# The last product of an mLSTM and feed-forward kernel: 256 tokens from seven products of halves for the second half of the tokens

## The chip, the cores and the metric

The kernel runs on one core of one Trainium2 chip. The metric is the device time of an execution in microseconds; smaller is better. A core has five engines that run their own instruction streams: PE (matrix products), DVE (vector), ACT (scalar), POOL (GpSimd) and SP (which here only issues DMAs). They wait for each other through semaphores.

## The reference

The input is q, k, v and an output gate of 4 batches x 8 heads x 768 tokens x 40, and two gates per token and head. An mLSTM cell is run over time, and its output, read as 3072 tokens of 320 features, goes through a multiplicative feed-forward net. All is in fp32.

```python
m_new = np.maximum(f_gate[:, :, t] + m, i_gate[:, :, t])
C = f_stab[:, :, None, None] * C + i_stab[:, :, None, None] * np.einsum('bhd,bhe->bhde', vt, kt)
h_tilde = np.einsum('bhde,bhe->bhd', C, qt)
denom = np.maximum(np.abs(nq), 1.0)
y[:, :, t] = o * h_tilde / denom
...
a = x @ w1            # x: 3072 x 320, w1 and w2: 320 x 1024
b = x @ w2
h = a * b @ w3        # 1024 x 1024
return (h @ w_out)    # 1024 x 320
```

## The kernel before

**Tiling.** The cell is worked in 24 chunks n of 128 tokens (n counts the four batches first, then time). A chunk is worked by step s = n: `quarter_work` makes the scores, the state products and, one step later, the outputs. The feed-forward net works on groups `gr` of four chunks, 512 tokens, six groups in all. `x_t[gr]` holds a group's cell output with features on the partitions. From `w3` and `w_out` the kernel first makes their product `w3o` (1024 x 320, as 8 slices of 128 rows; `w3_mm`), so that what is left of the net is (x w1 * x w2) w3o.

**The stages of the net.** For groups 0 to 2 `up` makes the products with w1 and w2 directly. For groups 3 to 5 `up_by_seven` makes them for 512 tokens by a scheme that needs seven products of halves in place of eight, with sums of the halves of the weights (`weight_sums`, on POOL, in steps 16 and 17) and of the tokens (`token_sums`, on DVE, line 647). It has four parts: `single` (three products per weight, line 674), `shared` (the other four, line 681, with copies by ACT, lines 688 and 690, and additions by DVE, lines 672, 670 and 697), `left` (the last 64 features and four additions by DVE, the "left additions", lines 670 and 672) and `product` (a times b, line 715). The result is `ab_t[gr]`, two tiles of 8 slices x 256 tokens, features on the partitions.

**The last product.** `ffn_out` (line 719) makes 128 tokens of the output: eight products of 128 x 128 weights (a slice of `ab_t`) with 320 columns of `w3o`, in one PSUM bank; ACT copies the bank (line 727) and issues the DMA to the output (line 729). There are 24 such blocks (`downs`).

**What sets the order.** The order is written out by hand. A loop runs over 32 steps; the lists `n_up`, `n_seven` and `n_down` say how many of the net's pieces each step holds:

```python
n_up = [0] * 2 + [1] * 4 + [2] * 10 + [0] * 16
n_seven = [0] * 19 + [1] * 12 + [0]
n_down = [0] * 16 + [2] * 5 + [1] * 9 + [0, 5]
```

Steps 0 to 23 carry the cell as well; step 24 (`s == NU`) finishes the last chunk's output; steps 25 to 31 hold the net alone. In steps 19 to 24 PE's order is `single`, `shared`, the blocks of `ffn_out`, `left`, then the cell's work; in steps 25 to 30 it is `shared`, `ffn_out`, `single`, `left`. PE's order is pinned (`in_order`), and the other engines work their streams in the order in which the compiler has put them, which follows the program's closely. On DVE a step runs: additions of `shared`, left additions, the cell's output for the chunk before (`outputs`, lines 412 to 434), `product`, the transpose of a chunk of x that has come back from DRAM (`x_turn`, line 461), and the transposes of the keys and queries of the chunk after (`turn`, line 313; they read the buffers `gates` and `q_all`, which the SP queue fills).

**PSUM.** Until step 24 two tiles of two banks each, `cell0` and `cell1`, belong to the cell and are lent to `shared`; four banks in rotation (`ps_m`) serve the rest. After step 24 the cell's banks are given to a second pool, and all eight go round in turn (`mps`): a product waits until the bank's last reader is done.

**Buffers.** `kbuf` (4 tiles), `vbuf` (5), `q_all` and `gates` hold the cell's inputs, and are not used after the last chunk. `pw` is a ring of five tiles for the cell's weights. `wo` is used again as `kept`, the intermediate sums of `up_by_seven`.

Of the kernel before, what the change touches and what calls it, by code (L numbers as in the profile page):

```python
# [8 lines left out]
FP = mybir.dt.float32  # L9
U32 = mybir.dt.uint32  # L10
AF = mybir.ActivationFunctionType
OP = mybir.AluOpType
# [4 lines left out]
def kernel(  # L17
# [26 lines left out]
    nc = tc.nc  # L44

    B, H, S, D = q.shape
# [30 lines left out]
    def mps(shape, name):  # L77
        pool = banks.pop(0)
        banks.append(pool)
        return pool.tile(shape, FP, name=name, tag="m")  # L80
# [29 lines left out]
    q_all = const.tile([P, NBQ * H * DP], FP, name="q_all")  # L110
    qbuf = [q_all[:, i * H * DP:(i + 1) * H * DP].rearrange("p (h d) -> p h d", d=DP) for i in range(NBQ)]
    kbuf = [const.tile([P, H, DP], FP, name=f"kbuf{i}") for i in range(NB)]
    vbuf = [const.tile([P, H, D1], FP, name=f"vbuf{i}") for i in range(NBV)]
    ident = const.tile([P, P], FP, name="ident")
    state = [[const.tile([P, NP, D1], FP, name=f"state{b}_{i}") for i in range(3)] for b in range(B)]
    aT = const.tile([P, NT2, BH], FP, name="aT")
# [132 lines left out]
    def fold():  # L249
        while ready_w3:  # L250
            w3_mm(ready_w3.pop(0))
        ready_w3.extend(turned_w3)
        turned_w3.clear()
# [465 lines left out]
    def ffn_out(blocks, pos=None):  # L719

        pos = pos or [mps([P, DM], "po") for _ in blocks]
        for (gr, j), po in zip(blocks, pos):
            for f in range(FO):
                mm(po, ab_t[gr][j // 2][:, f, j % 2 * P:(j % 2 + 1) * P], w3o[:, f, :], start=(f == 0), stop=(f == FO - 1))
        for (gr, j), po in zip(blocks, pos):
            o_sb = ffn.tile([P, DM], FP, name="o_sb", tag="o_sb", bufs=2)
            nc.scalar.copy(out=o_sb, in_=po)  # L727
            t0 = j * S + gr * P
            nc.scalar.dma_start(out=out[t0:t0 + P, :], in_=o_sb)


    ups = [(gr, [f, f + 1], slice(j * 2 * P, (j + 1) * 2 * P)) for gr in range(3) for j in range(2)
           for f in range(0, FO, 2)]
    downs = [(gr, j) for gr in range(NG) for j in range(GT)]
    sevens = [(gr, f) for gr in range(3, NG) for f in range(FH)]
    n_up = [0] * 2 + [1] * 4 + [2] * 10 + [0] * 16
    n_seven = [0] * 19 + [1] * 12 + [0]
    n_down = [0] * 16 + [2] * 5 + [1] * 9 + [0, 5]
    w12 = [("w12", i, part) for part in range(2) for i in range(2 * KF + 1)]
    todo = w12[5:] + [("wo", i, 0) for i in range(FO)] + [("w3", ko, part) for ko in range(FO) for part in range(2)]  # L740
    n_cvt = [0, 0, 2, 0, 1, 2, 3, 3, 3] + [2] * 6
# [5 lines left out]
    for s in range(len(n_up)):  # L747
# [28 lines left out]
        while s >= N_DVE and turned < min(s - 2, NY):  # L776
            x_trans(turned)
            turned += 1
        fold()
        seven = None  # L780
        if n_seven[s]:
            seven = up_by_seven(*sevens.pop(0), (lambda i: cell[i // 2][:, i % 2].rearrange("p (i t) -> p i t", i=2)) if s <= NU else
# [4 lines left out]
        if seven and s <= NU:  # L787
            ffn_out([downs.pop(0) for _ in range(n_down[s])], [cell[1][:, i, 0:DM] for i in range(2)])
        else:
            for _ in range(n_down[s]):  # L790
                ffn_out([downs.pop(0)])
        if seven and s > NU:
            seven[0]()
        now = [ups.pop(0) for _ in range(n_up[s])]
# [38 lines left out]
        with tc.issue_after(gated.ins) if gated else nullcontext():  # L833
            if seven:
                seven[3]()
            if NY <= s - 2 < NU:
                x_turn(s - 2)
            for n in () if s == 1 else (s + 2,) if s < B else (s + 2, s + 3) if s == B else (s + 3,):
                if n < N_U:
                    rows_of_u(n)  # L840
            if N_DVE <= s + 1 < NU:
                gated = turn(s + 1)
            if s - 2 in range(4 * GT - 1, NU, GT):
                token_sums((s - 2) // GT)
        if s == 0:
            weighted(1)
            weights(1)
            masks(1)
            gate_cols(g, gT, nc.scalar.copy)
# [37 lines left out]
            for ins in keep_order(front):  # L887
                behind.enter_context(tc.issue_after(ins))
    behind.close()
    assert not ups and not sevens and not downs and not todo and not pend and not turned_w3 and not ready_w3, (len(ups), len(downs), len(todo), len(pend))  # L890
# [1 line left out]
_INS = ['q', 'k', 'v', 'i_gate', 'f_gate', 'o_gate', 'moe_w1', 'moe_w2', 'moe_w3', 'moe_w_out']  # L892
_OUTS = [((3072, 320), 'float32')]
# [25 lines left out]
```

## Time and profile before

| | us |
|---|---|
| median of 3 executions | 436.54 (435.71 to 437.29) |
| the profiled execution | 436.73 |
| its span, first to last instruction | 435.0 |
| mean granted PE clock in it | 0.984 of full speed |
| PE busy | 421.6 (97%) |
| DVE busy | 306.3 (70%) |
| ACT busy | 151.8 (35%) |
| POOL busy | 92.8 (21%) |
| the products of `ffn_out` (po and cell<-w3o,ab) | 70.6 + 35.4 of PE |

Busy time is the time in which an engine works on an instruction; its share is over the whole span. A row of the profile names the line of the kernel, the engine, the operation, output<-inputs by the program's names and, in brackets, the idle time ahead of it with what ended it. An fp32 product appears as two records on PE, each with its own weight load on the row PEld. Records of PE overlap: the pace of a stream is read from starts, not from durations. The span ends with the last output DMA.

The steps are found by their products: step 20 lies at 264.8 to 283.4 us of the span, step 21 to 297.7, step 22 to 312.0, step 23 to 326.2, step 24 to 339.6, step 25 to 352.0; steps 26 to 29 take 12.43 each, step 30 ends at 409.9, and step 31 is the rest.

### The profile page before, as it was taken

How to read it: one execution, taken by the hardware profiler on the slowest of the kernel's cores; microseconds unless marked ns; L12 is line 12 of the kernel's file. 1: busy time of each engine (PE TensorE's matmuls, PEld its weight loads, DVE VectorE, ACT ScalarE, POOL GpSimd, SP SyncE). 2: the span in 40 equal slices, each digit the busy share in tenths (PEclk: the TensorE clock that was granted, in tenths of full speed). 3: DMA queues.
4: the chain of work that ended last, by engine and by line, in shares of the span. 5: the costliest groups of instructions: out<-in, count | busy, mean ns of one | idle time of the engine just before them, and what ended most of it. 6: DMA issues, size and time to landing. Idle time of an engine off the chain costs nothing.

```text
span 435.0 us, 12730 instructions
## 1 busy us (share of the span) xinstructions
PE 421.6 (97%) x5233; PEld 335.1 (77%) x5233; DVE 306.3 (70%) x633; ACT 151.8 (35%) x409; POOL 92.8 (21%) x163
## 2 busy tenths in 40 slices
PE   7699899999999999999999999999999999999996
PEld 6688778878788787887777778788777777777774
DVE  6756886778949778777746968698998876444800
ACT  4866563566724523530332203123211111110110
POOL 4530342333303203303317623022100000000000
PEclk9979799999999999999999999999999999999999
DMA  8999977498987776884426676746221110000001
GB/s 186 213 183 232 222 111 131 126 198 169 205 197 134 171 174 141 173 168 92 102 63 135 151 130 145 160 98 137 53 54 37 35 35 15 17 17 15 2 30 46
DMA packets 135211, 51.14 MB, mean 118 GB/s; under 512 B 109360, under 2 KB 126960, under 8 KB 135152
## 3 DMA queue, kind: packets, MB, share of 16 engines
q1 hardware_dynamic: 131552, 46.29, 51.7%
q10 hardware_dynamic: 3600, 4.03, 2.7%
q8 instruction: 41, 0.67, 0.7%
q14 instruction: 18, 0.15, 0.1%
HBM read 44.50 MB, written 5.80 MB: 116 GB/s over the span
## 4 chain that ended last, share of the span: by engine, by line
PE 71%; SPq 8%; issue 8%; DMA 5%; POOL 3%; DVE 2%; ACT 1%; POOLq 0%; DVEq 0%; ACTq 0%
PE cell L92 19%; PE pa L92 19%; PE pb L92 12%; PE po L92 10%; PE wp L92 6%; PE p L92 5%; SPq L135 4%; DMA raw<-in_moe_w_dram 3%; SPq L180 2%; POOL pw L304 1%; POOL raw L645 1%; SPq L149 1%; SPq L144 1%; DVE w3T L652 1%; PE pt L95 1%
## 5 line engine op out<-in xcount | busy, mean ns | idle before, releaser
L92 PE MATMUL po<-w3o,ab 128*128 128x320 f32 x256 | 70.6, 433 | 0.0
L92 PEld LDWEIGHTS po<-w3o,ab 128*128 128x128 f32 x256 | 48.4, 190 | 19.7 <-issue 0.4
L92 PE MATMUL pa<-xT,w 128*128 128x256 f32 x240 | 61.5, 387 | 1.6 <-ACT xT L475 1.6
L331 POOL TENSOR_TENSOR state<-state,decay 128x164 f32<-128x164 f32 x40 | 19.7, 493 | 168.9 <-DVE state L395 139.2
L92 PEld LDWEIGHTS pa<-xT,w 128*128 128x128 f32 x240 | 45.3, 194 | 9.5 <-ACT xT L475 2.1
L299 ACT ACTIVATE pw<-pw,aT 128x64 f32<-128x64 f32 x184 | 46.4, 339 | 3.3 <-ACT o_sb L727 1.9
L304 POOL TENSOR_SCALAR_AFFINE_SELECT pw<-pw 64x512 f32<-64x512 f32 x48 | 38.2, 796 | 37.0 <-ACT pw L299 24.7
L92 PE MATMUL pb<-xT,w 128*128 128x256 f32 x192 | 45.4, 379 | 0.0
L92 PEld LDWEIGHTS pb<-xT,w 128*128 128x128 f32 x192 | 36.5, 190 | 5.0
L92 PE MATMUL pa<-xT,wr 64*64 64x256 f32 x384 | 37.0, 386 | 0.5 <-DVE wr L196 0.5
L92 PE MATMUL pb<-xT,wr 64*64 64x256 f32 x384 | 36.4, 380 | 0.0
L92 PE MATMUL wp<-wo,w3T 128*128 128x320 f32 x128 | 35.9, 433 | 0.2
L624 ACT ACTIVATE a_sb<-pa 128x512 f32<-128x512 f32 x24 | 14.3, 596 | 61.5 <-PE pb L92 61.5
L92 PE MATMUL cell<-w3o,ab 128*128 128x320 f32 x128 | 35.4, 432 | 0.0
L625 DVE TENSOR_TENSOR ab<-pb,a_sb 128x512 f32<-128x512 f32 x24 | 16.4, 686 | 25.8 <-ACT a_sb L624 25.7
L727 ACT COPY o_sb<-po 128x320 f32<-128x320 f32 x16 | 6.8, 426 | 74.4 <-PE po L92 74.4
L92 PEld LDWEIGHTS cell<-w3o,ab 128*128 128x128 f32 x128 | 24.3, 190 | 9.5
L672 DVE SCALAR_TENSOR_TENSOR a_sb<-pa,wo 128x512 f32<-128x512 f32 x12 | 8.3, 690 | 32.6 <-PE pa L92 32.6
L92 PEld LDWEIGHTS wp<-wo,w3T 128*128 128x128 f32 x128 | 23.8, 190 | 9.6 <-DVE ab L625 0.4
L92 PEld LDWEIGHTS pa<-xT,wr 64*64 64x64 f32 x384 | 18.9, 132 | 15.4 <-issue 8.8
L419 DVE TENSOR_TENSOR h<-cell,h 64x164 f32<-64x164 f32 x88 | 28.7, 326 | 1.7
L92 PEld LDWEIGHTS pb<-xT,wr 64*64 64x64 f32 x384 | 20.1, 133 | 3.0
(141 smaller groups left out, 730.4 us busy)
## 6 DMA issues: line engine op xcount, KB each, us to landing
raw<-in_moe_w_dram SPq DMA_DIRECT2D x64, 128.0 KB, 3.2
kbuf<-in_k_dram SPq DMA_DIRECT2D x24, 160.0 KB, 4.2
vbuf<-in_v_dram SPq DMA_DIRECT2D x24, 160.0 KB, 4.7
o_in<-in_o_gate_dram SPq DMA_DIRECT2D x24, 160.0 KB, 4.8
out_dram<-o_sb ACTq DMA_DIRECT2D x24, 160.0 KB, 1.8
pw<-U_d SPq DMA_DIRECT2D x28, 128.0 KB, 3.6
raw<-in_moe_w_dram SPq DMA_DIRECT2D x5, 512.0 KB, 6.8
raw<-in_moe_w_out_dram SPq DMA_DIRECT2D x8, 320.0 KB, 3.8
```

The lines of the kernel that those rows point to most:

```text
L92: in_order(nc.tensor.matmul(out, lhsT=lhsT, rhs=rhs, start=start, stop=stop))
L95: in_order(nc.tensor.transpose(out, in_, ident[0:n, 0:n]))
L135: nc.sync.dma_start(out=dst, in_=rows(src, n))
L180: nc.sync.dma_start(out=dst, in_=src)
L299: nc.scalar.activation(out=pw[:, h, :], in_=src[:, h, :], func=AF.Exp, bias=aT[:, c, b * H + h:b * H + h + 1])
L304: nc.gpsimd.affine_select(out=pw[r], in_=pw[r], compare_op=OP.is_ge, fill=0.0, base=0, pattern=[[0, H], [1, L]], channel_multiplier=-1)
L331: nc.gpsimd.tensor_tensor(out=new, in0=old, op=OP.mult, in1=decay[:, b * NP:(b + 1) * NP, 2 * c + x:2 * c + x + 1] .to_broadcast([P, NP, D1]))
L419: nc.vector.tensor_tensor(out=part, in0=ph[x][halves[e]], in1=part, op=OP.add)
L624: nc.scalar.mul(out=a_sb, in_=pa, mul=UP ** -2)
L625: nc.vector.tensor_tensor(out=ab_t[gr][j][:, fs[0]:fs[-1] + 1, t0:t0 + a_sb.shape[-1]], in0=pb, in1=a_sb, op=OP.mult)
L672: nc.vector.scalar_tensor_tensor(out=out, in0=p, scalar=UP ** -2, in1=q, op0=OP.mult, op1=OP.add)
L727: nc.scalar.copy(out=o_sb, in_=po)
```

## The change

For groups 3 to 5 the last product is made for 256 tokens at once (`out_by_seven`). The 256 x 1024 block of `ab` and the 1024 x 320 matrix `w3o` are each cut into four quarters, and seven products of quarters (each 128 tokens x 512 x 160, four slices of 160 columns) are made in place of eight. They need

- four differences of quarters of `w3o` (`out_weight_sums`), made once by POOL in step 24's code, in the buffers `gates` and `q_all`;
- four sums of quarters of `ab` for each 256 tokens (`ab_sums`), made by DVE, in the `kbuf` tiles or in four tiles of the ring `pw`: at the end of the step before the one that needs them, and for the last three at the top of steps 30 and 31 and behind step 31's first product;
- the merging of the seven results: a copy by ACT and five additions by DVE into `o2`, a part of what was `vbuf` and is now one tile `v_all`, from which ACT issues two DMAs.

The order of the blocks changes with it. Groups 0 to 2 keep their 12 blocks of 128 tokens, two a step in steps 16 to 19 and one in steps 20 to 23; before, steps 16 to 20 held two, steps 21 to 29 one, and step 31 five. The six new blocks of 256 tokens stand in steps 25, 27 and 29, one each, and in step 31, three.

```diff
--- before.py
+++ after.py
@@ -110,7 +110,8 @@
     q_all = const.tile([P, NBQ * H * DP], FP, name="q_all")
     qbuf = [q_all[:, i * H * DP:(i + 1) * H * DP].rearrange("p (h d) -> p h d", d=DP) for i in range(NBQ)]
     kbuf = [const.tile([P, H, DP], FP, name=f"kbuf{i}") for i in range(NB)]
-    vbuf = [const.tile([P, H, D1], FP, name=f"vbuf{i}") for i in range(NBV)]
+    v_all = const.tile([P, NBV * H * D1], FP, name="v_all")
+    vbuf = [v_all[:, i * H * D1:(i + 1) * H * D1].rearrange("p (h d) -> p h d", d=D1) for i in range(NBV)]
     ident = const.tile([P, P], FP, name="ident")
     state = [[const.tile([P, NP, D1], FP, name=f"state{b}_{i}") for i in range(3)] for b in range(B)]
     aT = const.tile([P, NT2, BH], FP, name="aT")
@@ -729,13 +730,71 @@
             nc.scalar.dma_start(out=out[t0:t0 + P, :], in_=o_sb)
 
 
+    KH, NH = FO // 2, DM // 2
+
+    def out_weight_sums():
+
+        T_o.extend(m[:, i * KH * NH:(i + 1) * KH * NH].rearrange("p (f n) -> p f n", n=NH)
+                   for m in (gates, q_all) for i in range(2))
+        (B11, B12), (B21, B22) = ([w3o[:, k * KH:(k + 1) * KH, i * NH:(i + 1) * NH] for i in range(2)] for k in range(2))
+        T1, T2, T3, T4 = T_o
+        for dst, p, q in ((T1, B12, B11), (T2, B22, T1), (T3, B22, B12), (T4, B21, T2)):
+            nc.gpsimd.tensor_tensor(out=dst, in0=p, in1=q, op=OP.subtract)
+
+    T_o, S_o = [], {}
+
+    def quarters_of_ab(gr, j):
+        return [[ab_t[gr][j][:, k * KH:(k + 1) * KH, t * P:(t + 1) * P] for k in range(2)] for t in range(2)]
+
+    def ab_sums(gr, j):
+        mem = [t.rearrange("p h d -> p (h d)") if j == 0 else io.tile([P, H, L], FP, name="pw", tag="pw", bufs=5)
+               .rearrange("p h t -> p (h t)") for t in kbuf]
+        S1, S2, S3, S4 = S_o[gr, j] = [t.rearrange("p (f t) -> p f t", t=P) for t in mem]
+        (A11, A12), (A21, A22) = quarters_of_ab(gr, j)
+        for dst, p, q, op in ((S1, A21, A22, OP.add), (S2, S1, A11, OP.subtract), (S3, A11, A21, OP.subtract),
+                              (S4, A12, S2, OP.subtract)):
+            nc.vector.tensor_tensor(out=dst, in0=p, in1=q, op=op)
+
+    def out_by_seven(gr, j, sums=None):
+
+
+        (A11, A12), (A21, A22) = quarters_of_ab(gr, j)
+        S1, S2, S3, S4 = S_o[gr, j]
+        (B11, B12), (B21, B22) = ([w3o[:, k * KH:(k + 1) * KH, i * NH:(i + 1) * NH] for i in range(2)] for k in range(2))
+        T1, T2, T3, T4 = T_o
+        o2 = v_all[:, j * DM * 2:(j + 1) * DM * 2].rearrange("p (i n) -> p i n", n=NH)
+
+        def products(pairs, name):
+            po = mps([P, len(pairs), NH], name)
+            for i, (a, b) in enumerate(pairs):
+                for f in range(KH):
+                    mm(po[:, i], a[:, f, :], b[:, f, :], start=(i == f == 0), stop=(i == len(pairs) - 1 and f == KH - 1))
+            return po
+
+        p15 = products(((A11, B11), (S1, T1)), "o15")
+        nc.scalar.copy(out=o2[:, 0:4:3], in_=p15)
+        p67 = products(((S2, T2), (S3, T3)), "o67")
+        p23 = products(((A12, B21), (S4, B22)), "o23")
+        p4 = products(((A22, T4),), "o4")
+        for i in range(2):
+            nc.vector.tensor_tensor(out=o2[:, 1 + i], in0=p67[:, i], in1=o2[:, i], op=OP.add)
+        nc.vector.tensor_tensor(out=o2[:, 1:4:2], in0=o2[:, 1:3], in1=o2[:, 3:4].to_broadcast([P, 2, NH]), op=OP.add)
+        nc.vector.tensor_tensor(out=o2[:, 0:2], in0=p23, in1=o2[:, 0:2], op=OP.add)
+        nc.vector.tensor_tensor(out=o2[:, 2:3], in0=p4, in1=o2[:, 2:3], op=OP.add)
+        for t in range(2):
+            t0 = (2 * j + t) * S + gr * P
+            nc.scalar.dma_start(out=out[t0:t0 + P, :], in_=o2[:, 2 * t:2 * t + 2].rearrange("p i n -> p (i n)"))
+
     ups = [(gr, [f, f + 1], slice(j * 2 * P, (j + 1) * 2 * P)) for gr in range(3) for j in range(2)
            for f in range(0, FO, 2)]
-    downs = [(gr, j) for gr in range(NG) for j in range(GT)]
+    downs = [(gr, j) for gr in range(3) for j in range(GT)]
+    outs = [(gr, j) for gr in range(3, NG) for j in range(2)]
+    summed = list(outs)
     sevens = [(gr, f) for gr in range(3, NG) for f in range(FH)]
     n_up = [0] * 2 + [1] * 4 + [2] * 10 + [0] * 16
     n_seven = [0] * 19 + [1] * 12 + [0]
-    n_down = [0] * 16 + [2] * 5 + [1] * 9 + [0, 5]
+    n_down = [0] * 16 + [2] * 4 + [1] * 4 + [0] * 8
+    n_out = [0] * 25 + [1, 0, 1, 0, 1, 0, 3]
     w12 = [("w12", i, part) for part in range(2) for i in range(2 * KF + 1)]
     todo = w12[5:] + [("wo", i, 0) for i in range(FO)] + [("w3", ko, part) for ko in range(FO) for part in range(2)]
     n_cvt = [0, 0, 2, 0, 1, 2, 3, 3, 3] + [2] * 6
@@ -777,6 +836,10 @@
             x_trans(turned)
             turned += 1
         fold()
+        if s == NU:
+            out_weight_sums()
+        if s >= len(n_up) - 2:
+            ab_sums(*summed.pop(0))
         seven = None
         if n_seven[s]:
             seven = up_by_seven(*sevens.pop(0), (lambda i: cell[i // 2][:, i % 2].rearrange("p (i t) -> p i t", i=2)) if s <= NU else
@@ -789,6 +852,10 @@
         else:
             for _ in range(n_down[s]):
                 ffn_out([downs.pop(0)])
+        for i in range(n_out[s]):
+            out_by_seven(*outs.pop(0))
+            if summed and n_out[s] > 1:
+                ab_sums(*summed.pop(0))
         if seven and s > NU:
             seven[0]()
         now = [ups.pop(0) for _ in range(n_up[s])]
@@ -842,6 +909,8 @@
                 gated = turn(s + 1)
             if s - 2 in range(4 * GT - 1, NU, GT):
                 token_sums((s - 2) // GT)
+            if s + 1 < len(n_up) - 1 and n_out[s + 1]:
+                ab_sums(*summed.pop(0))
         if s == 0:
             weighted(1)
             weights(1)
@@ -887,7 +956,7 @@
             for ins in keep_order(front):
                 behind.enter_context(tc.issue_after(ins))
     behind.close()
-    assert not ups and not sevens and not downs and not todo and not pend and not turned_w3 and not ready_w3, (len(ups), len(downs), len(todo), len(pend))
+    assert not ups and not sevens and not downs and not outs and not summed and not todo and not pend and not turned_w3 and not ready_w3, (len(ups), len(downs), len(todo), len(pend))
 # ---- launch: one core; inputs and outputs as the reference has them ----
 _INS = ['q', 'k', 'v', 'i_gate', 'f_gate', 'o_gate', 'moe_w1', 'moe_w2', 'moe_w3', 'moe_w_out']
 _OUTS = [((3072, 320), 'float32')]
```

The diff has one line that only checks the lists at the end.

## The prediction

> **What bounds the kernel now.** I read the page first, then the stages, then the instructions in order of time around one step. On the page:
>
> ```profile
> PE 421.6 (97%) x5233; PEld 335.1 (77%) x5233; DVE 306.3 (70%) x633; ACT 151.8 (35%) x409; POOL 92.8 (21%) x163
> PEclk9979799999999999999999999999999999999999
> ```
>
> PE is occupied 97% of 435.0 us, and the second line shows the granted clock falling in two early slices. The stages that the change touches (columns: stage, its length, then busy us and instructions of PE, weight loads, DVE, ACT, POOL, then clock, DMA share, GB/s), with steps 20, 23, 24, 25, 27 and the last step, after a stage from early on:
>
> ```profile
> 44.56:47.97 3.41, 1.37 (x27) 0.69 (x29) 3.30 (x11) 3.41 (x12) 0.00 (x0) 1.00 1.05 176
> 47.97:51.39 3.42, 3.42 (x129) 3.34 (x126) 2.92 (x7) 0.13 (x1) 3.14 (x5) 0.50 1.02 365
> 51.39:54.80 3.41, 3.41 (x14) 3.23 (x15) 3.17 (x11) 2.02 (x5) 0.48 (x3) 0.50 0.99 144
> ...
> 264.84:283.42 18.58, 18.58 (x211) 14.52 (x205) 14.44 (x29) 4.31 (x14) 4.73 (x6) 1.00 0.74 146
> 311.96:326.24 14.28, 14.28 (x193) 11.46 (x189) 13.10 (x28) 1.97 (x4) 1.17 (x3) 1.00 0.19 42
> 326.24:339.58 13.34, 13.34 (x143) 10.52 (x140) 10.21 (x25) 1.50 (x3) 0.00 (x0) 1.00 0.20 44
> 339.58:352.02 12.44, 12.44 (x84) 9.41 (x77) 9.60 (x22) 1.61 (x3) 0.00 (x0) 1.00 0.22 46
> 364.45:376.89 12.44, 12.44 (x81) 9.41 (x77) 6.68 (x12) 1.61 (x3) 0.00 (x0) 1.00 0.04 14
> 409.89:435.00 25.11, 21.80 (x84) 15.11 (x80) 3.08 (x5) 2.13 (x5) 0.00 (x0) 1.00 0.09 34
> ```
>
> From step 20 on PE never stops, so a microsecond of PE work is a microsecond of time. But in step 23 DVE works 13.10 of 14.28 us: what hides DVE there is PE's length, and the change shortens PE. Steps 24 and 25 in order of time:
>
> ```profile
> 332.65 0.88 DVE L672 SCALAR_TENSOR_TENSOR wo<-cell,wo 128x256 f32<-128x256 f32 x2 [0.50 <-PE cell L92]
> ...
> 343.14 4.47 PE L92 MATMUL po<-w3o,ab 128*128 128x320 f32 x16
> ...
> 345.29 0.57 DVE L461 STREAM_TRANSPOSE xT<-yb 128x384 f32<-128x384 f32 x1
> 345.78 0.84 DVE L672 SCALAR_TENSOR_TENSOR wo<-p,wo 128x256 f32<-128x256 f32 x2
> ```
>
> PE begins the last product of step 25 at 343.14, while DVE finishes step 24's work only at 345.8. Today nothing on PE needs it. Then two rows on shared memory and one on a short product:
>
> ```profile
> 242.88 1.44 POOL L645 TENSOR_TENSOR raw<-w 128x512 f32<-128x512 f32 x1
> 243.23 1.37 DVE L652 TENSOR_TENSOR w3T<-xT,w3T 128x256 f32<-128x256 f32 x1
> ```
>
> ```profile
> 22.54 2.34 PE L92 MATMUL fill<-ident 128*128 128x128 f32 x10
> ```
>
> The L652 op takes 0.42 us when POOL is idle (step 25) and 1.37 here: it ends 0.3 us after POOL's.
>
> **What the Trainium skill says.** "SBUF — State Buffer", section "SBUF: two separate sides": a DVE operation with two SBUF inputs and a GpSimd operation exclude each other for whole instructions. The rows above agree; operations with one PSUM input keep their 0.32 us beside POOL. "TensorE: Matmul & The Clock Gate", Part 1: the clock is halved after a little-used window of about 3.4 us, and the windows run free of the program. The trace agrees on the length: a stretch with PE busy 1.37 of 3.41 us is followed by two stretches at 0.50. Same page, "LDWEIGHTS": a load costs its columns / 1.2 GHz, an estimated 107 ns for 128; no row shows a load's true occupancy (190 ns are recorded beside each 320-column record), but the fill row bounds it.
>
> **The change, part by part.** Times are on the old time axis; an fp32 product is two records.
>
> *PE work.* A 320-column record goes at 4.31/16 = 0.269 us, a 256-column one at 0.216 (0.43 for two). On that line 160 columns are 0.135. Eight blocks' two-record products for 256 tokens: 32 x 0.269 = 8.62. Seven of halves: 7 x 4 x 2 = 56 x 0.135 = 7.58. Six times 1.04: **-6.2 us**. The unknown is the weight load, now 56 in place of 32, under shorter products. Fill (128 columns, new weights each time, half clock) goes at (2.34-0.42)/9 = 0.213 us, exactly 128 columns at half rate, so the load hides under 0.107 us at full clock if it scales. I take 0.135. Lower end: no gain beyond this. Upper end: the recorded 0.190 us, 10.6 us each, +12 us in all.
>
> *Moved work.* Step 20 and step 24 lose one 4.31 us block each; steps 25, 27, 29 hold 7.58 in place of 4.31, steps 26 and 28 nothing; the last step three sevens for five blocks. In step 20 DVE waited 3.22 us for PE (the wait before its left additions at 280.83), so it is about 0.9 us late after the move; step 21's waits (0.89 + 0.17) take that up. I charge 0.15 us for one bank (L419 to the next shared product has 0.7 us of room).
>
> *POOL, four differences of w3o (128x640).* By L645's 1.28 us for 512 columns, about 1.6 each. They stand behind the last decay (312.8): two into gates at 313.3 to 316.6, two into q_all once the turn of step 22's end has read it (about 321 to 325). Nothing queues behind them on POOL. DVE operations with two SBUF inputs meet them: L432 (1.1 us late), L697 twice (0.8 + 0.6), less the 0.86 that DVE waits at 323.65 and 324.52: DVE enters step 24's cell work about 1.5 us late, and 1.0 of it remains at the shared additions (333.6 in place of 332.65). At the low end nothing meets: 0.
>
> *DVE, the sums of ab (four 128x512).* By L697, 0.69 each; in a row 0.73+0.61+0.61+0.61 = 2.6 us, six times. They are in front of the next step's shared additions. Merging a seven: 0.36+0.36+0.53+0.41+0.32 = 2.0 us. From step 26 on DVE has the room: per pair of steps 2 x 6.68 + 4.6 = 17.9 of 23.9 us. The narrowest place is step 27, where S1 is ready some 0.2 us before PE asks; I charge 0.
>
> *The new wait.* Step 25's seven needs S1 after its first product, and DVE makes S1 after everything of step 24: from the shared additions 3.0, left additions 2.4, the cell's outputs 3.5, product 1.2, transpose 0.5, that is 10.6 us, and S1 0.7. With 333.6 for the start S1 is there at 344.9; its load, 345.1. PE has lost step 24's block: shared product at 329.7 (0.8 late: cell1 is freed by late L419), left and cell work until 336.1; step 25's shared product needs the pa bank, freed by DVE at 337.4 (**1.3 us wait**); it ends at 340.9, the first product of the seven at 342.0; **3.1 us wait** for S1. Everything behind on PE's one queue waits with it. Sum 0.8 + 1.3 + 3.1 = +5.2. Then DVE is ahead again: shared additions need PE only later, and no PSUM bank comes round late.
>
> *Tail.* The last copy on ACT (0.43) becomes one DVE addition of 160 columns (0.32); both DMAs of a pair wait on ACT's queue for DVE, with only next copies behind them, which are not yet due: -0.1. The ACT copies (0.43) of o15 take the place of the old ones. vbuf as one tile: the same loads with the same waits, 0.
>
> Sum without a change of clock: 6.2 + 0.1 - 0.15 - 5.2 = 1.0 us less, span 434.0. Span 435.0 belongs to an execution of 436.73; the median is 436.54, and I take differences from it: **435.5**.
>
> *The clock.* A stop of 3.1 us, 1.3 us of another shortly before, is as poor a stretch as 44.56. If a free-running window covers some 2.4 us of it (about half of the positions: (3.41 + 3.1 - 2 x 2.4)/3.41), the next 3.4 us, perhaps 6.8, go at half rate: 1.7 (3.4) us lost, **437.2** (438.9). The forecast is the middle of executions of both kinds, **436.4**: the gain on PE is given back at step 25. Its own range 435.0 to 437.8.
>
> **The rivals.**
> - *The gain stands* (434.3 or less): POOL's differences meet DVE in nothing (-1.0) and the clock holds: 436.54 - 2.0 = 434.5. For it: such meetings turn on tenths of a microsecond. Against: L652 shows the lock, and even without it S1 comes 2 us after PE needs it.
> - *The clock falls for two stretches*: 438.9, slower. For it: both falls in the trace lasted 6.83 us. Against: PE's next stretch is full-width work.
> - *The weight load is the bound* (slower, the other sign): above 8.62/56 = 0.154 us a record the sevens cost more than the eights; at 0.190, 12 + 5.2 gives about 453; at 0.16, +2 with the waits: 443. For it: the recorded 190 ns. Against: the fill row, and 64x41 quadrant products whose four loads of 64 columns go by in 0.05 us.
> - *It does nothing new*: excluded, other products are issued; six sevens stand in PE's order.
>
> **How the numbers follow.** Forecast (435 to 437.8) 0.50; gain stands 0.20; two stretches 0.17; weight load 0.07; waits that I did not find (late transposed y, a bank) 0.06. 0.3% is 1.3 us, about what a measurement of this kernel can tell from no change. Faster (under 435.2): most of the second and a little of the first, 0.20. Slower (over 437.8): third, fourth, fifth and a little of the first, 0.34. Same 0.46. Range: 433.9 from the second, 440.0 past the third; the weight load is left out above.
>
> **What would show it.** Right: 160-column records 0.135 us apart; PE idle about 3 us before the first product of o15 with kbuf, ended by DVE's ab sums (L756 of the new kernel), and about 1 us before step 25's p15; POOL's w3o differences beside a stretched L432/L433 and L697/L698; half clock just after, in some executions. Wrong: a pace over 0.154; no stop in step 25; stops in steps 27 to 31.

## The result and the profile after

The changed kernel takes 438.76 us (median of 20 executions, 435.83 to 442.06), the kernel before 436.25 us (20 executions beside them, 434.16 to 438.03). The ratio is 1.0053, with a 95% interval of 1.0033 to 1.0074: slower by half a per cent, 2.4 us above the forecast of 436.4. That is above the 435.0 to 437.8 of the forecast's main case, inside its whole range of 433.9 to 440.0, and on the side that it gave 0.34. The profiled execution took 437.64 us, its span 435.8.

From the page of the changed kernel, the engines' busy time and the granted clock:

```profile
PE 416.5 (96%) x5377; PEld 343.4 (79%) x5377; DVE 336.1 (77%) x687; ACT 149.4 (34%) x403; POOL 100.1 (23%) x167
PEclk9969999999999999999999999999999899999999
```

PE is busy 5.1 us less and DVE 29.8 us more. The clock line has a new digit 8 in its slice from 338 to 349 us. Stretches of the changed kernel (stage, length, busy us of PE, weight loads, DVE, ACT, POOL, clock, DMA share, GB/s): steps 23, 24 and 25, then the 3.41 us before S1 and the 3.41 after:

```profile
307.17:322.51 15.34, 14.80 (x191) 11.28 (x188) 15.02 (x28) 1.97 (x4) 7.23 (x7) 1.00 0.24 51
322.51:333.38 10.87, 9.38 (x128) 7.40 (x125) 10.56 (x26) 1.07 (x2) 0.00 (x0) 1.00 0.18 33
333.38:353.66 20.28, 17.68 (x116) 15.44 (x116) 14.68 (x32) 1.61 (x3) 0.00 (x0) 0.92 0.17 40
...
337.26:340.67 3.41, 1.12 (x8) 0.87 (x7) 3.31 (x8) 0.00 (x0) 0.00 (x0) 1.00 0.17 27
340.67:344.08 3.41, 3.11 (x12) 3.14 (x13) 3.31 (x7) 0.43 (x1) 0.00 (x0) 0.50 0.38 70
```

In steps 23 and 24 DVE works nearly the whole length and PE no longer does: they have changed places. In the kernel before DVE had room: its three longest waits in steps 20 to 24 were these, all for PE's left products:

```profile
280.83 0.69 DVE L672 SCALAR_TENSOR_TENSOR a_sb<-pa,wo 128x512 f32<-128x512 f32 x1 [3.22 <-PE pa L92]
...
295.11 0.69 DVE L672 SCALAR_TENSOR_TENSOR a_sb<-pa,wo 128x512 f32<-128x512 f32 x1 [0.89 <-PE pa L92]
...
337.93 0.69 DVE L672 SCALAR_TENSOR_TENSOR a_sb<-pa,wo 128x512 f32<-128x512 f32 x1 [2.15 <-PE pa L92]
```

In the changed kernel none of the three is left. Its rows from step 23 to step 25 in order of time:

```profile
310.03 1.54 POOL L742 TENSOR_TENSOR gates<-w3o,gates 128x640 f32<-128x640 f32 x1
310.27 1.33 DVE L428 TENSOR_SCALAR den<-h 128x8 uint32<-128x8 uint32 x1
310.29 0.70 PE L92 MATMUL cell<-xT,w 128*128 128x256 f32 x2 [0.26 <-DVE h L420]
...
312.56 1.99 PE L92 MATMUL cell<-w3T,raw 128*128 128x256 f32 x8 [0.28 <-DVE state L396]
...
318.03 2.00 DVE L698 TENSOR_TENSOR wo<-wo 128x512 f32<-128x512 f32 x1
...
325.77 0.70 PE L92 MATMUL cell<-xT,w 128*128 128x256 f32 x2 [0.40 <-DVE h L420]
...
333.38 0.70 PE L92 MATMUL p<-xT,w 128*128 128x256 f32 x2 [1.09 <-DVE a_sb L673]
...
340.22 0.65 DVE L756 TENSOR_TENSOR kbuf<-ab 128x512 f32<-128x512 f32 x1
340.97 3.94 PE L92 MATMUL o<-gates,kbuf 128*128 128x160 f32 x16 [2.60 <-issue]
```

L742 are POOL's differences of `w3o`; beside them a DVE operation of 0.17 us takes 1.33 and one of 0.69 takes 2.00. PE stops twice in step 23, once in step 24, at step 25's shared product (333.38) and at S1 (340.97; the profile names no releaser, but L756 has made S1 0.1 us earlier). Stops measured between starts are a little longer than the bracketed idle time: 0.43, 0.45, 0.57, 1.28 and 2.76 us. After the last one, sixteen records of 160 columns take 3.94 us; in e12 below, where no stop comes before them, they take 2.44. The difference is the half clock.

The two profiles compared by step, with what the blocks alone account for (a block 4.31, a seven 7.58 us) and what is left over:

| step | before | after | blocks and sevens | left over | in the forecast |
|---|---|---|---|---|---|
| 20 | 18.58 | 14.27 | -4.31 | 0.00 | |
| 21 | 14.27 | 14.43 | 0 | 0.16 | 0.15 |
| 22 | 14.27 | 14.28 | 0 | 0.01 | 0 |
| 23 | 14.28 | 15.34 | 0 | **1.06** | 0 |
| 24, with step 25's first wait | 13.34 | 10.87 | -4.31 | **1.84** | 0.8 + 1.3 |
| 25 | 12.44 | 20.28 | +3.27 | **4.57** | 3.1, clock 0.85 |
| 26 to 29 | 49.74 | 47.73 | -2.08 | 0.07 | 0 |
| 30 | 8.13 | 8.13 | 0 | 0.00 | 0 |
| 31 to the end | 25.12 | 26.32 | +1.19 | 0.01 | -0.1 |
| sum | 170.17 | 171.65 | -6.24 | 7.72 | 6.1 |

So the profile is 1.48 us longer from step 20 on. The forecast's 6.24 us of saved PE work are there; 7.72 are given back.

### The profile page after: what moved, and what is told of

Same layout as the page of the kernel before. It is cut to its first block, busy times and chain, and to the rows that moved or that the text cites. A ratio compares the mean times of both kernels' runs of the same rounds, so it can differ in the third digit from the quotient of the medians.

```text
span 435.8 us, 13100 instructions
## 1 busy us (share of the span) xinstructions
PE 416.5 (96%) x5377; PEld 343.4 (79%) x5377; DVE 336.1 (77%) x687; ACT 149.4 (34%) x403; POOL 100.1 (23%) x167
## 4 chain that ended last, share of the span: by engine, by line
PE 71%; issue 12%; DVE 8%; POOL 5%; DMA 2%; ACT 1%; SPq 0%; DVEq 0%; POOLq 0%; ACTq 0%
PE pa L92 18%; PE cell L92 15%; PE pb L92 12%; PE o L92 11%; PE wp L92 6%; PE p L92 5%; POOL pw L305 2%; POOL raw L646 1%; PE px L95 1%; DVE w3T L653 1%; PE pt L95 1%; POOL state L332 1%; DVE h L420 1%; DVE pw L389 1%; DMA pw<-U_d 1%
## 5 line engine op out<-in xcount | busy, mean ns | idle before, releaser
L92 PEld LDWEIGHTS pa<-xT,w 128*128 128x128 f32 x240 | 44.4, 190 | 8.7 <-ACT xT L476 2.1
L420 DVE TENSOR_TENSOR h<-cell,h 64x164 f32<-64x164 f32 x88 | 28.7, 326 | 1.7
L92 PE MATMUL cell<-w3o,ab 128*128 128x320 f32 x96 | 26.7, 432 | 0.0
L92 PE MATMUL po<-w3o,ab 128*128 128x320 f32 x96 | 26.4, 433 | 0.0
L92 PEld LDWEIGHTS po<-w3o,ab 128*128 128x128 f32 x96 | 18.1, 190 | 7.3
L92 PEld LDWEIGHTS cell<-w3o,ab 128*128 128x128 f32 x96 | 18.2, 190 | 7.1
L413 DVE TENSOR_TENSOR h<-cell,gT 128x328 f32<-128x328 f32 x24 | 11.8, 490 | 14.3 <-PE cell L92 14.3
L691 ACT ACTIVATE wo<-p 128x512 f32<-128x512 f32 x6 | 3.6, 598 | 51.3 <-PE p L92 38.6
```

The costliest lines, as they stand in the source:

```text
L92: in_order(nc.tensor.matmul(out, lhsT=lhsT, rhs=rhs, start=start, stop=stop))
L413: nc.vector.tensor_tensor(out=h.rearrange("p (n two) d -> p two n d", two=2), in0=pi, in1=gT[:, c, hs].rearrange("p (n two) -> p two n", t ...
L420: nc.vector.tensor_tensor(out=part, in0=ph[x][halves[e]], in1=part, op=OP.add)
```

## The experiments

All were timed beside the kernel before. In the expectations T1 is the account under test; T2, T3 and "rival" are others. Because the first 198 us differ between executions whatever the kernel (step 15 begins at 196.3 to 200.5 us), profiles are compared from step 15's first product to the end of the span: 237.2 us before, 238.7 after.

| run | median | before beside it | ratio (95%) | profile from step 15, against before |
|---|---|---|---|---|
| e1 the change again | 438.72 | 437.03 | 1.0030 (1.0014 to 1.0046) | +1.5 |
| e2 PE kept busy at S1 | 437.55 | 437.03 | 1.0017 (0.9996 to 1.0037) | +0.4 |
| e3 order within the sevens | 436.84 | 437.03 | 0.9982 (0.9959 to 1.0004) | -0.3 |
| e4 group 3 in blocks | 434.02 | 437.03 | 0.9927 (0.9902 to 0.9952) | -3.0 |
| e5 no differences of w3o | 437.28 | 436.88 | 1.0013 (0.9990 to 1.0035) | +1.0 |
| e6 new order, blocks only | 439.86 | 436.88 | 1.0064 (1.0041 to 1.0086) | +2.8 |
| e7 e4, differences on DVE | 433.09 | 436.88 | 0.9922 (0.9896 to 0.9947) | -4.1 |
| e8 five sevens | 434.87 | 436.88 | 0.9951 (0.9928 to 0.9974) | -3.0 |
| e9 a block back in step 24 | 435.21 | 437.71 | 0.9946 (0.9928 to 0.9965) | -1.8 |
| e10 a block back in step 20 | 437.11 | 437.71 | 0.9999 (0.9981 to 1.0018) | +1.0 |
| e11 five sevens, second form | 433.53 | 437.71 | 0.9904 (0.9872 to 0.9937) | -3.5 |
| e12 six sevens, both blocks back | 436.78 | 437.88 | 0.9982 (0.9963 to 1.0002) | +1.3 |

A single profile and a median can differ by one or two us (e10 and e12 above all), so the profiles are used for where the time goes, and the ratios for how much.

### e1 and e2: is it the clock?

e1 is the changed kernel unchanged.

> The changed kernel once more, beside the kernel before on the same chip. Clock theory (T1): the stop of 2.8 us in step 25 often takes the clock down after it, in more executions and for longer than the forecast had it, so the runs of the changed kernel have a lower mean granted clock than those of before, by 0.004 to 0.008 (one to two stretches of 3.41 us at half rate in a span of 436 us: 3.41 x 0.5 / 436 = 0.0039 each), and the ratio is again 1.003 to 1.007. Rival (T2): the time is lost in waits or transfers that the profile shows at full clock; then the mean clocks of both kernels are alike, and the profile has stops outside steps 23 to 25.

e2 puts work without use into the stop at S1:

```diff
...
             for i, (a, b) in enumerate(pairs):
+                if (gr, j) == (3, 0) and name == "o15" and i == 1:
+                    bank67.append(mps([P, 2, NH], "o67"))
+                    for _ in range(9):
+                        mm(bank67[0].rearrange("p i n -> p (i n)")[:, 0:P], ident, ident)
                 for f in range(KH):
...
```

> The changed kernel with nine products of the identity by itself put between A11 B11 and S1 T1 of step 25's seven, into a bank that is overwritten afterwards: 18 records of 128 columns, about 18 x 0.107 = 1.9 us of PE in the 2.8 us in which it stood still for S1. No wait gets shorter. T1 (the clock): the half-rate stretch after 340.7 us is gone from the profile, the mean clock rises by 0.002 to 0.006, and the median falls by 1 to 2 us (ratio to before 0.999 to 1.003). T2 (the clock there doesn't matter): 438.8 as before, ratio 1.005.

e1 repeats the result, and its profile has the same stops and the same half-rate stretch. The clock is lower by less than expected: 0.9865 against 0.9885 as a mean of the executions beside each other, which is half a stretch of 3.41 us in each execution, and too little to be told from none. The executions' clocks don't tell how often the stretch comes: in e5 and e10, which have the same stop, they are lower than before's by 0.5 and 0.3 stretches, and in e7 and e8, which have no such stop, by about one. In e2, rows in order of time around S1 and the page's clock line:

```profile
338.87 2.17 PE L92 MATMUL o<-ident 128*128 128x128 f32 x18
341.63 1.73 PE L92 MATMUL o<-gates,kbuf 128*128 128x160 f32 x11 [0.59 <-issue]
```

```profile
PEclk9979999999999999999999999999999999999999
```

S1 is as late as before, but the half-rate stretch is gone, and the median is 1.2 us below e1's (the two ratios' intervals overlap, so the size rests on the profile). T1 holds: the clock after the stop is a part of the loss, 1.6 us in the profile (twelve records 0.132 us too slow). It is not all of it, since e2 is no faster than before, with the whole saving on PE.

### e3: less waiting for S1

```diff
-        p15 = products(((A11, B11), (S1, T1)), "o15")
...
+        for po, i, n, a, b in ((p15, 0, 2, A11, B11), (p23, 0, 2, A12, B21), (p4, 0, 1, A22, T4), (p15, 1, 2, S1, T1)):
+            for f in range(KH):
+                mm(po[:, i], a[:, f, :], b[:, f, :], start=(i == f == 0), stop=(i == n - 1 and f == KH - 1))
         nc.scalar.copy(out=o2[:, 0:4:3], in_=p15)
...
```

> In every seven the three products that need least (A11 B11, A12 B21, A22 T4) come first and S1 T1 fourth, so that 2 x 8 records of 160 columns, 2 x 1.08 = 2.2 us, stand before the wait for S1. T1: the wait falls from 2.8 to about 0.6 us (-2.2) and with it the half-rate stretch after it in most executions (another 1 to 1.7 us): 434.9 to 435.6, ratio about 0.998. T2: -2.2 from the wait and nothing else: 436.6, ratio 1.000. A third reading (T3: what comes before S1 is only moved, and DVE's later work of step 25 sets the end): nothing gained, 438.8.

The ratio is what T1 said, and step 25 alone won 3.7 us (12.0 from its first product to its first `single` product, 15.7 after): the stop fell to 0.54 us and the clock held. But 1.9 us went elsewhere. The new order puts S4 B22 last, so all of DVE's additions come after PE's end: 1.07 us more from the last product to the end of the span. And step 22 took 15.14 us. What e3's trace answers on DVE's transposes of y (L462) in steps 20 to 22 (us in sum, number of times):

```profile
its engine sat idle before it (us, times) until:
  DMA yb<-y_d: 2.0, 1
```

This is a wait that the forecast had named and not priced. The cell's y is sent to DRAM and read back, and DVE's transpose of it (`x_turn`) is in front of DVE's next work. The kernel before never waits for it in steps 20 to 24. In the kernels with one block less in step 20 it often does, and step 22, in which PE needs a bank that DVE then frees later, grows with it:

| | after | e1 | e2 | e5 | e6 | e3 |
|---|---|---|---|---|---|---|
| DVE waits for y in step 21 | 0 | 0.92 | 1.00 | 1.07 | 1.20 | 2.03 |
| step 22 over its 14.27 us | 0.01 | 0.17 | 0.37 | 0.44 | 0.60 | 0.87 |

The profile of the changed kernel has only a wait of 0.27 us for y, in step 22; e1 is the same kernel, so this differs between executions.

### e4: sevens only where DVE has time

```diff
...
-    n_down = [0] * 16 + [2] * 4 + [1] * 4 + [0] * 8
-    n_out = [0] * 25 + [1, 0, 1, 0, 1, 0, 3]
+    n_down = [0] * 16 + [2] * 5 + [1] * 6 + [0] * 5
+    n_out = [0] * 27 + [1, 0, 0, 0, 3]
```

> Group 3 stays in blocks of 128 tokens (two a step in steps 16 to 20, one in steps 21 to 26); only groups 4 and 5 are made from seven products (steps 27 and three in 31). Four times 1.04 = 4.2 us of PE are saved in place of 6.2; DVE has 12 us of room before the first S1. T1 and the sum of the prediction: no stop at S1, none at step 25's p15, no half-rate stretch there: 436.3 - 4.2 + 0.2 = 432.3, ratio 0.990 to 0.993. T2 (what is lost has to do with the sevens, their sums, merges and DMAs wherever they stand): a gain under 1.5 us, ratio over 0.996.

T1: the ratio is 0.9927, and no stop is left in steps 25 to 31. So the sevens, their sums, mergings and DMAs are worth what they save when they stand there. Of 4.16 us the profile has 3.0; the missing 1.1 are in steps 23 and 24 (see e7).

### e5 and e6: POOL's part, and the part of moving

e5 makes no differences (`for dst, p, q in ():`), e6 keeps the new order and makes plain blocks:

```diff
-    n_down = [0] * 16 + [2] * 4 + [1] * 4 + [0] * 8
-    n_out = [0] * 25 + [1, 0, 1, 0, 1, 0, 3]
+    n_down = [0] * 16 + [2] * 4 + [1] * 4 + [0, 2, 0, 2, 0, 2, 0, 6]
+    n_out = [0] * 32
...
```

> The changed kernel without POOL's four differences of w3o: nothing is computed for them, their buffers keep old data, and all else is issued as it was. T1, as refined by the step lengths of the first runs (from step 22 to S1 DVE never waits, so what DVE loses there PE loses too): DVE's L428 and L698 are 1.2 + 1.3 = 2.5 us shorter, step 23 takes about 14.4 in place of 15.34 us, S1 is ready 1 to 2.5 us earlier, and the median falls from 438.7 to between 436.2 and 437.7 (ratio 0.999 to 1.0015; the half-rate stretch may stay, since PE still stops for about 2 us at S1). Rival: DVE has slack there and POOL costs nothing: 438.7, ratio 1.003 to 1.005.

> The changed order with plain blocks of 128 tokens: two in steps 25, 27 and 29 each and six in step 31, no sevens, no sums, no differences of w3o, so neither S1 nor POOL is in the way. T1: the blocks taken from steps 20 and 24 were what PE worked on while DVE caught up; without them PE waits 0.2 in step 21, about 0.5 in step 24 and up to 1.3 us at step 25's shared product, and nothing saves: 436.8 to 438.3, ratio 1.000 to 1.003, no half-rate stretch. Rival (T4: the moved blocks cost by themselves as much as the whole change): over 438.5, ratio 1.004 or more.

e5 came out in T1's range by its ratio, but the size was less than expected: step 23 took 14.90, not 14.4, and S1 came 0.7 us earlier, counted from step 15. The stop there was as long as ever (2.72 us, with its half-rate stretch), because both of step 25's stops hang on DVE: once PE has waited for it at the shared product, the way to S1 is the same on both engines (7.54 us, 7.59 in the changed kernel). In this trace the profile names the releaser of the stop:

```profile
340.43 1.88 PE L92 MATMUL o<-gates,kbuf 128*128 128x160 f32 x8 [2.55 <-DVE kbuf L756]
```

e6 went to the rival: 439.86 us, a ratio at least as high as that of the change itself, with no seven, no sum and no difference in it. Its steps 22, 23 and 24:

```profile
294.20:309.07 14.87, 14.54 (x192) 11.37 (x188) 14.52 (x33) 3.88 (x12) 2.53 (x5) 1.00 0.57 117
309.07:323.85 14.78, 14.54 (x193) 11.37 (x189) 13.98 (x30) 1.97 (x4) 1.15 (x3) 1.00 0.25 54
323.85:334.05 10.20, 9.11 (x127) 7.48 (x124) 9.39 (x24) 1.07 (x2) 0.00 (x0) 1.00 0.21 40
```

Steps 21 to 24 lose 0.16 + 0.60 + 0.51 + 1.17 = 2.4 us by the move alone, for 3.1 in the changed kernel: POOL's share is 0.6 net. T1 had put the price of the move at up to 1.3 us (ratio 1.000 to 1.003). That was wrong: it had nothing for steps 22 and 23, which lose 1.1. The two blocks taken from steps 20 and 24 were what PE worked on while DVE and the way of y through DRAM caught up.

### e7: the differences on DVE

e4, with `nc.vector` in place of `nc.gpsimd` in `out_weight_sums` and its call moved to the end of step 25.

> As the kernel with group 3 in blocks, but the four differences of w3o are made by DVE at the end of step 25 in place of POOL in steps 23 and 24. T1: of the 4.16 us that four sevens save, POOL's differences gave back 1.1 (step 23 took 14.71 for 14.27, step 24 14.01 for 13.34); DVE has 2.4 to 3.4 us of waiting in each of steps 26 and 27 for four operations of about 0.85 us. So step 23 and 24 are as in the kernel before, nothing else changes, and the median falls from 434.0 to 432.9 (ratio 0.990). Rival: DVE's own differences make S1 late in step 27: no better than 434.0, with a stop on S1.

Steps 23 and 24 of e4, then of e7:

```profile
312.50:327.21 14.71, 14.54 (x192) 11.37 (x188) 14.39 (x26) 1.97 (x4) 7.27 (x7) 1.00 0.20 44
327.21:341.22 14.01, 13.61 (x143) 10.44 (x140) 11.38 (x27) 1.50 (x3) 0.00 (x0) 1.00 0.19 42
```

```profile
312.11:326.38 14.27, 14.27 (x191) 11.45 (x188) 13.10 (x28) 1.97 (x4) 1.17 (x3) 1.00 0.20 42
326.38:339.73 13.35, 13.35 (x144) 10.53 (x140) 10.23 (x25) 1.50 (x3) 0.00 (x0) 1.00 0.21 44
```

With 6.1 us of work taken from POOL, DVE's busy time in step 23 falls by 1.29 and PE has no stop left. On DVE the four differences take 0.82 us each, and the profile gains 1.08 us, for 1.1 expected. The ratio to before hardly differs from e4's (0.9922, 0.9927): the two intervals cover each other, so the gain of e7 over e4 rests on the profile.

### e8 and e11: five sevens

Both make the second half of group 3 from seven products too, and so have 14 plain blocks; as in e7, DVE makes the differences. e8 leaves step 16 without a block, e11 leaves one there and moves two sevens a step later:

```diff
-    n_down = [0] * 17 + [2] * 4 + [1] * 6 + [0] * 5
-    n_out = [0] * 27 + [1, 0, 1, 0, 3]
+    n_down = [0] * 16 + [1] + [2] * 4 + [1] * 5 + [0] * 6
+    n_out = [0] * 28 + [1, 0, 1, 3]
```

> As the last, but with five sevens: the second half of group 3 (256 tokens) is made from seven products too, in step 27, one more follows in step 29, three in step 31; the 14 blocks left stand two a step in steps 17 to 20 and one in steps 21 to 26, and step 16 has none (DVE works 4.9 of 12 us there). T1: 5 x 1.04 = 5.2 us saved, 0 to 0.5 lost in step 16: 431.9 to 432.4, ratio 0.988 to 0.989. Rival: step 16 without its blocks makes the next chunks' loads or DVE late: 433 or more.

> Five sevens as before, DVE making the differences of w3o, with one block in step 16 (none there in the first form of it), two each in steps 17 to 20, one each in steps 21 to 25, none from step 26; sevens in steps 28 and 30 and three in step 31. T1: the PE stop of 1.2 us in step 16 and the 0.8 us before step 20 were what the missing blocks of step 16 cost, and one block is enough there: 5 x 1.04 = 5.2 us saved, 431.6 to 432.3, ratio 0.988. Rival: step 16 needs both blocks, or DVE falls behind in steps 26 and 27 that hold neither blocks nor sevens: 433 or more.

e8 was the rival's: PE stops 1.23 us in step 16, waiting for DVE's transposed queries, and 0.82 ahead of step 20; these 2.1 us are what was missing from 5.2. In e11 both are gone, and a 0.36 us stop in step 27 and one of 0.92 at the first seven's S1 are there in their place: 3.45 us gained in the profile, ratio 0.9904. With 433.53 us e11 fell on its rival's side as well, for the second reason that this named: DVE is late in step 27. It and e7 beat both kernels; which of the two is better is not told apart.

### e9 and e10: which of the two missing blocks

The changed kernel with one block more in step 24, or in step 20, and one less in step 16:

```diff
-    n_down = [0] * 16 + [2] * 4 + [1] * 4 + [0] * 8
+    n_down = [0] * 16 + [1] + [2] * 3 + [1] * 5 + [0] * 7
```

```diff
-    n_down = [0] * 16 + [2] * 4 + [1] * 4 + [0] * 8
+    n_down = [0] * 16 + [1] + [2] * 4 + [1] * 3 + [0] * 8
```

> The changed kernel, all six sevens, with one of its twelve plain blocks put back into step 24, taken from step 16 (one there, two each in steps 17 to 19, one each in steps 20 to 24). From step 20 to S1 DVE hardly waits in the changed kernel (0.9 us in all between 264 and 341 us), so time is lost there only as far as PE gets ahead of DVE. T1: 4.31 us more of PE work in step 24 fill the stops at step 25's shared product and at S1 (1.28 + 2.76 us) and there is no half-rate stretch (1.6); what was lost in steps 21 to 23 (1.2) and at step 24's p15 (0.6) stays: 438.7 - 4.0 - 1.2 to 1.6 = 433.1 to 433.5, ratio 0.990 to 0.993. Rival (the block is missed in step 16): at least 1.2 us worse, 434.7 or more, with a PE stop in step 16.

> The same with the block put back into step 20 in place of step 24 (one in step 16, two each in steps 17 to 20, one each in 21 to 23). T1: in step 20 DVE waits 3.2 us for PE again, behind the two blocks, so of the 4.31 us only about 1.1 us reach S1; the stops of step 25 and the half-rate stretch stay, and only the losses of steps 21 and 22 go: 437.3 to 438.0, ratio 1.000 to 1.003. Rival (a block is worth the same wherever it stands ahead of S1): about 433.5, as the other kernel.

e10 went as T1 said. There is no wait for y, steps 21 and 22 take 14.27 us, and both stops of step 25 (1.28 and 2.76) and the half-rate stretch are untouched. Step 23 takes 14.71 us in place of 15.34, as in e4, so 0.63 of its 1.06 us came from the missing block and 0.43 from POOL. Steps 21, 22 and 23 of e10:

```profile
278.49:292.76 14.27, 14.27 (x190) 11.45 (x189) 13.02 (x28) 4.51 (x15) 3.12 (x5) 1.00 0.64 122
292.76:307.03 14.27, 14.27 (x191) 11.45 (x188) 13.92 (x32) 3.88 (x12) 2.42 (x4) 1.00 0.43 96
307.03:321.74 14.71, 14.55 (x193) 11.38 (x189) 14.39 (x26) 1.97 (x4) 7.25 (x7) 1.00 0.19 40
```

The profile is 0.5 us shorter than that of the changed kernel, the ratio lower by 0.3 to 0.5%; the difference is not explained. In e9 the stop at the shared product is gone, but T1 was wrong about S1: 2.31 us of stop remain. The block stands ahead of `left`, so DVE waits 2.14 us for PE's left products in step 24, and from DVE's left additions S1 is as far away as ever (8.5 us, 8.2 in the changed kernel). So the ratio, 0.9946, is short of T1's 0.990 to 0.993. The median of 435.21 lies on the rival's side, but the rival's stop in step 16 is not there. The clock held all the same. Two stretches of e9, cut at whole multiples of 3.413 us from a change of the clock in the same execution (at 30.58 us):

```profile
337.78:341.19 3.41, 2.59 (x15) 2.16 (x14) 3.23 (x9) 0.40 (x1) 0.00 (x0) 1.00 0.00 0
341.19:344.61 3.42, 2.10 (x15) 2.13 (x16) 3.39 (x7) 0.42 (x1) 0.00 (x0) 1.00 0.41 66
```

The stop is shared between two of them, and neither is poor enough; in the changed kernel one held 1.12 us of PE work and the next went at half rate.

### e12: everything put back

Blocks in steps 20 and 24 again, one block less in each of steps 16 and 17, and e3's order in step 25's seven alone.

> All six sevens, with every cover that the runs so far showed to be missing put back: the blocks of steps 20 and 24 stand again (one block each in steps 16 and 17 in place of two), and only in step 25's seven the three products that need no S come before S1 T1 (in the other sevens the order stays, so that the tail is that of the changed kernel). The account of the runs so far: the block in step 20 gives the transposed y time to come back (no wait of DVE in step 21, steps 21 and 22 at 14.27), the block in step 24 fills step 25's shared product's stop, two products of 1.09 us fill the 2.3 us stop at S1 to 0.1. Left are POOL's differences in steps 23 and 24 (0.44 + 0.67 in the kernel with group 3 in blocks) and 0.2 in the pace of the sevens: -6.24 + 1.4 = -4.8 us, ratio 0.988 to 0.990. Rival (step 17, where DVE works 6.8 us and PE is left 6.8, becomes DVE's, or the account has a hole): ratio 0.992 or more.

It was the rival. In part the account held: steps 21 and 22 take 14.27 and 14.28 us, and PE goes through S1 without a stop. Step 23 did not fit it: it takes 15.34 us again, where 14.7 were expected. And the stretch from step 15 to step 20 grew by 5.5 us over its work. Rows from step 17 on (DVE, then PE):

```profile
234.35 0.58 DVE L462 STREAM_TRANSPOSE xT<-yb 128x384 f32<-128x384 f32 x1 [2.68 <-DMA yb<-y_d]
...
236.94 0.69 PE L92 MATMUL cell<-qT,kT 40*64 40x64 f32 x32 [1.12 <-DVE qT L314]
...
248.10 0.58 DVE L462 STREAM_TRANSPOSE xT<-yb 128x384 f32<-128x384 f32 x1 [3.83 <-DMA yb<-y_d]
```

It is y again: one step is cut to 6.80 us (216.1 to 222.9), the way through DRAM no longer fits, and DVE waits 2.7, 3.8, 4.8 and 1.4 us for it at its next four transposes, the last in step 21, with PE behind it. So DVE comes late into the steps that follow; that this is why step 23 is long again is argued, not shown. A half-rate stretch at 239 us comes with it in this profile, behind this stretch:

```profile
235.64:239.05 3.41, 2.04 (x81) 1.47 (x72) 3.38 (x7) 2.38 (x9) 2.31 (x3) 1.00 0.81 188
```

A block can be taken from step 16 (e9, e10, e11 lose nothing there), not from step 17 as well.

## Why the prediction was wrong

It forecast no change and it is slower by 0.5% (0.3% in e1). Its mechanism, that the gain on PE is given back at step 25, was right, but not complete. Against the profile its sum was 1.6 us too small: 1.06 us in step 23 and 0.75 of clock were missing, and other terms, mostly the stops, were together 0.2 too large. The profile shows 1.5 us of loss, the ratio of the first measurement 2.3; what makes up the rest is open.

- *PE work: right.* Records of 160 columns start 0.135 us apart (eight in 1.09 us, also after new weights each time), a seven takes 7.60 us. The weight load is no bound; that rival fell.
- *The stops of steps 24 and 25: right in place.* 0.8, 1.3 and 3.1 us were forecast, 0.57, 1.28 and 2.76 measured, at the places named and ended by DVE's work. That the sizes fit is luck in part: the forecast had 1.0 us of lateness from POOL's differences in them, and e5, without the differences, has the same stops of 1.28 and 2.72. There is no stop from step 26 on, and no bank comes round late. The tail is as forecast: 3.32 us from the end of the last record to the end of the span before, 3.24 after.
- *"Step 21's waits take that up. I charge 0.15 us for one bank": the step that failed.* Step 21 did lose 0.16 us, as charged. But the lateness from step 20 was followed through this one step and taken as settled. In the kernel before, DVE's waits in steps 20 to 24 sum to 8.6 us; in the changed kernel 0.9 is left from step 20 to S1, and none from step 23 on. With that room gone what is late on DVE is late on PE too, and steps 22 and 23 have it at nothing in the forecast. Step 23 lost 1.06 us: 0.63 by the move, as e10 shows, which has the block of step 20 back, and 0.43 by POOL's differences, the same as in e4. Without the differences the move takes 1.1 us from steps 22 and 23 (e6; e5 as well), so the two do not simply add. The row at 310.29 is the move's: PE waits for L420 before POOL has held DVE up. The row at 312.56 is POOL's: L396 stands behind L428. The late y, which the forecast named and did not price, comes on top in some executions (0.9 us of DVE's time in e1); with the block of step 20 back it is not there (e10).
- *POOL's differences: right in kind, partly in place.* They were forecast to meet L432 and L697; they met L428 (1.33 for 0.17 us) and L698, the old L697 (2.00 for 0.69), 2.5 us on DVE as the forecast's own sum of stretches (1.1 + 0.8 + 0.6). "The Trainium skill", page "SBUF — State Buffer", section "SBUF: two separate sides", says that a GpSimd operation and a DVE operation with two SBUF inputs or in a two-port mode take the shared ports for a whole instruction; e7 agrees, where both steps go back to their old lengths. The forecast let them cost PE nothing in step 23 and 1.0 us at S1; the net price on PE was 0.6 us in the changed kernel (e5, e6), none of it at S1, and 1.1 in e4.
- *The clock: right in kind, its condition too strict.* The forecast asked that a stretch of 3.41 us have some 2.4 us of the stop in it, which gave "about half of the positions" and 0.85 us in the mean. Its own row at 44.56 has PE idle for 2.04 us and half rate behind it. With 1.77 us, the least idle time of the stretches in these traces that were all followed by half rate (see the last section), and the measured stop of 2.76 us, the same formula gives an estimate of (3.41 + 2.76 - 2 x 1.77)/3.41, about 0.77 of the positions and 1.3 us. All four profiles in which the stop stood whole (after, e1, e5, e10) have the half-rate stretch behind it; how often it comes in other executions stays open. The price of a stretch, 1.6 to 1.7 us, was right. By taking the middle of two kinds of executions as the forecast, I gave the number of neither: its own sum for an execution with the stretch was 437.2.

## What to carry to other kernels

Work that hides another engine's lateness is not free to move: before a block is taken out of a step, sum the other engine's waits over that step and all that follow until it has room again, and look at every round trip (here y through DRAM) that the shorter step no longer covers. A new dependence is best put where its producer has room (e4, e7), or behind independent products of its own consumer (e3), and two thirds or five sixths of the saving on PE (e4, e7, e11) then gain 0.7 to 1%, where the whole of it lost 0.5%. Where a stop of PE of nearly 3 us is expected, count the half-rate stretch behind it as part of its price.

## What the runs showed of the hardware

- The half-rate stretch follows how poor one counted stretch of 3.41 us is, not the stop itself. With PE busy 0.81 to 1.36 us of it (e10, e5, after, e1) the next was at half rate; with 2.10 and 2.59 us (e9, the stop cut in two) or with 1.9 us of products without use put into it (e2) it was not. In all 14 traces, cut into such stretches at the changes of the clock, the 13 at full rate with PE busy under 1.7 us (0.81 to 1.64) were all followed by half rate. From 1.7 to 2.4 us both happen: 2.04 us in e12, with small products of 40 and 64 rows, was followed by it. So busy time alone does not settle it there.
- A DVE operation with a single small input in SBUF (L428, 128x8, and in e4 and e10 also L430) was held by POOL's 128x640 subtraction: 1.33 and 1.10 us in place of 0.17 and 0.16. It ends within 0.03 us of POOL's. The forecast had looked for operations with two such inputs only.
- Four differences of 128x640 take 1.54 us each on POOL and 0.82 on DVE (e7).
